# Reordering the first batch of a fused linear-attention and mixture-of-experts kernel

## The chip, the cores and the metric

The kernel runs on one core of one Trainium2 chip. The metric is the device time of one execution in microseconds (us), so lower is better. The core has five engines with a queue each: TensorE for matmuls (PE in the profile, with its weight loads as PEld), VectorE (DVE), ScalarE (ACT), GpSimd (POOL) and SyncE (SP). Work moves between HBM and on-chip memory by DMA transfers, which an engine's queue issues. Every engine goes through its own queue in order.

## The reference, cut to what matters

Attention with a cosine weighting is followed by a mixture of experts whose gates are balanced by eight Sinkhorn steps. Eight batches of eight heads, 576 positions and 64 features each make 4608 tokens of 512 features.

```python
theta = np.pi / 2.0 * pos / S
def phi(x, c, s):
    r = np.maximum(x, 0.0)
    return np.concatenate([r * c, r * s], axis=-1)
q_p, k_p = phi(q, cos_w, sin_w), phi(k, cos_w, sin_w)
kv = np.einsum('bhsf,bhsd->bhfd', k_p, v)       # "key sums with values"
z = np.sum(k_p, axis=2)                         # "key sums"
num = np.einsum('bhsf,bhfd->bhsd', q_p, kv)     # numerators
den = np.einsum('bhsf,bhf->bhs', q_p, z)[..., None] + 1e-06   # denominators
x = num / den                                   # tokens of the experts
...
P = np.exp(x @ w_gate - max)                    # then 8 rounds of row and column scaling
for e in range(E):                              # E = 8
    out += P[:, e:e + 1] * (np.maximum(x @ w1[e], 0.0) @ w2[e])
```

## The kernel before

All matmul operands are 16-bit floats; the loads from HBM convert from 32-bit on the way. The kernel has two phases. In the first, the eight batches go through the attention one by one, and the first expert's two layers run between their pieces, so that TensorE is never without work: block `j` of the first expert handles 512 tokens in 16 slots (eight slots `ffn1`, one for each 128 columns of the first layer, then eight half tiles of `ffn2`), and the table `todo` puts pieces of batch `j + 1` behind the slots. In the second phase the other seven experts run back to back. This change touches only what comes ahead of that regular rhythm: the first batch (batch 0), and the preparation of batch 1 up to slot 4 of block 0.

Work on TensorE, VectorE and ScalarE keeps the order in which the code issues it: each goes through an `InOrder` wrapper (line 109 of the profile, which is why nearly all rows carry L109, and why rows are told apart by their tiles). What a written position says is therefore what the engine does. GpSimd issues the loads of q, k, v and of the weights (`load` at L202, `load_w1` at L127, `load_w2` at L133), in written order too. These issues share eight completion semaphores in turn, so that the ninth and every later issue waits until the issue eight places earlier has landed. Each q, k or v load brings half a batch (two of four head pairs `hk`); the first layer's weights come in four quarters of 256 columns, and so do those of the second layer.

The steps that the prediction names, by function and by the tiles that the profile shows:

- `prep_q(b, hk)`: VectorE scales a head pair's queries by cosine and sine, `q_p<-q_ld,acc_hi` (the table `cs` lives in `acc_hi`). `qp_pool` has three buffers.
- `turn(b, hk, i)`: TensorE transposes a third of it by a matmul with the identity, `small_ps<-ident,q_p`; ScalarE or VectorE writes it to `q_pT` with the relu (for batch 1's last two head pairs the target lies in `acc_lo` and `acc_hi`).
- `prep_k` applies the relu to the keys in place (`k_ld<-k_ld`; by ScalarE for head pairs 0 and 1 of batch 1), `prep_kp` scales them on VectorE (`k_p<-k_ld,acc_hi`).
- `key_sums` sums batch 0's keys by 36 small matmuls from the table `cs_half` (`small_ps<-cs_half,k_ld`), `key_sums_made` spreads them into `zsel`.
- `denominators` multiplies `zsel` with `q_pT` into a bank named `y_ps`; behind head 7, VectorE takes the reciprocal and splits it into two 16-bit parts (`den`, `hi`, `hl`).
- `sums_begun` and `sums_made` sum keys with values (`small_ps<-v_ld,k_p`, then `kv_sb` by ScalarE), two head pairs at a time.
- `spread_out` spreads the reciprocals over the features (`small_ps<-hl,acc_hi`, then `rb` by ScalarE), `numerators` multiplies `q_pT` with `kv_sb`, and VectorE multiplies the product with `rb` into `xT`. `attend` is both.
- the first L1: the first layer of the first 512 tokens for column groups 0 to 3, accumulated over `kt = hk` as the head pairs of `xT` come ready; ScalarE applies the relu into `hT`.
- `keep_busy(n)`: matmuls of ones (dummies) of n times 128 columns, whose result nobody reads.

The banks called `small_ps` are four, used in turn. The order in which the first batch is written (L610 to L638) is this:

```python
for hk in range(HK):
    if hk == 3:
        prep_k(0, 0); prep_k(0, 1)
        z_ps = key_sums(0)
        prep_q(0, hk)
        key_sums_made(0, z_ps)
    else:
        prep_q(0, hk)
    for i in range(3):
        turn(0, hk, i, True)
        keep_busy(3)
```

Behind it stand the scaled keys, the denominators and the sums, and then a loop over `hk` that holds `attend(0, hk)`, the first L1 of the head pair before, and one or two scaled keys of batch 1.

Of the kernel before, what the change touches and what calls it, by code (L numbers as in the profile page):

```python
# [19 lines left out]
XS = 64.0  # L20
# [5 lines left out]
def kernel(  # L26
# [154 lines left out]
    with ExitStack() as p1:  # L181
# [16 lines left out]
        def load(b, half, names="qkv", held_back=False):  # L198
            for name in names:
                x = ld.tile([P, 2, C, D], F16, name=f"{name}_ld")  # L200
                view = sources[name][b].rearrange("(hk hh) (p c) d -> (hh p) hk (c d)", hh=2, c=C)
                i = nc.gpsimd.dma_start(  # L202
                    out=x[:].rearrange("p hk c d -> p hk (c d)"),
                    in_=view[:, 2 * half : 2 * half + 2],
                )
                if held_back:

                    after(ve.last, i)
                landing[name, b, half] = i
                for i in range(2):  # L210
                    loaded[name, b, 2 * half + i] = x[:, i]
# [3 lines left out]
        ve.memset(half_pi[:], float(np.pi / 2.0))  # L215
        ang = float(np.pi / (2.0 * S))
        load(0, 0, "q")
        gidx = cs_pool.tile([P, C], FP32, name="gidx")
        nc.gpsimd.iota(
            gidx[:], pattern=[[1, C]], base=0, channel_multiplier=C,  # L220
            allow_small_or_imprecise_dtypes=True,
        )

        ones_sq = cs_pool.tile([P, P], F16, name="ones_sq")
        ve.memset(ones_sq[:], 1.0)
        ident = cs_pool.tile([P, P], F16, name="ident")
# [1 line left out]
            out=ident[:], in_=ones_sq[:], pattern=[[-1, P]], compare_op=ALU.is_equal,  # L228
            fill=0.0, base=0, channel_multiplier=1,
        )  # L230
        load(0, 1, "q")
        for name in "kv":
            load(0, 0, name)
            load(0, 1, name)
        w0 = new_weights(wA)
        load_w1(w0, 0, 4, (0, 1))
        load(1, 0, "k")
# [7 lines left out]
        def keep_busy(n):  # L245

            for cols in [TCH] * (n // 4) + [n % 4 * P] * (n % 4 > 0):
                te.matmul(
                    out=idle_ps[:, 0:cols],
                    lhsT=ones_sq[:],  # L250
                    rhs=ones_sq[:, 0:1].to_broadcast([P, cols]),
                    start=True,
                    stop=True,
                )

        idle_ps = ps_y.tile([P, Dm], FP32, name="y_ps")
        for _ in range(74):
            keep_busy(1)

        wrap = cs_pool.tile([P, C], FP32, name="wrap")  # L260
# [12 lines left out]
        se.activation(out=cs[:, :, 1, :], in_=s_b, func=AF.Sin, scale=ang)  # L273
        cs_half = cs_pool.tile([P, C, 2, 2], F16, name="cs_half")
        ve.memset(cs_half[:], 0.0)
        for hh in range(2):
            ve.tensor_copy(
                out=cs_half[hh * HP : (hh + 1) * HP, :, :, hh],
                in_=cs[hh * HP : (hh + 1) * HP, :, :, 0],
            )  # L280
        early = cs_pool.tile([P, 1], FP32, name="early")
        se.activation(out=early[:], in_=half_pi[:], func=AF.Exp)

# [3 lines left out]
        for h in range(H):  # L287
            ve.memset(zmask[:, h, h : 32 : H], 1.0)
        C3 = C // 3

        lo = cs_pool.tile([P, 1], FP32, name="lo")

# [4 lines left out]
        with nc.allow_low_precision("sums of zeros and ones"):  # L297
# [8 lines left out]
            out=spread.rearrange("p j hk hh d -> p (j hk hh) d"),  # L306
            in_=sel[:].rearrange("p j h -> p (j h)").unsqueeze(2).to_broadcast([P, 3 * H, D]),
        )
        ones_col = const.tile([P, 1], FP32, name="ones_col")
        ve.memset(ones_col[:], 1.0)  # L310
        ones_all = const.tile([P, P], FP32, name="ones_all")
        ve.memset(ones_all[:], 1.0)
        eps_row = cs_pool.tile([1, 32], FP32, name="eps_row")
        ve.memset(eps_row[:], 1e-6 / XS)
        wg_ld = cs_pool.tile([P, KT, E], FP32, name="wg_ld")
        nc.sync.dma_start(out=wg_ld[:], in_=moe_w_gate.rearrange("(kt p) e -> p kt e", p=P))
        wg = const.tile([P, KT, E], F16, name="wg")
# [2 lines left out]

        kps, qps, qTs, kvs, hls = {}, {}, {}, {}, {}

        lent = acc_lo[:, G_LO - 4 : G_LO, :].rearrange("p g d -> p (g d)").bitcast(F16)
        VA = C * (D + 2)
        v_augs = [
            lent[:, i * VA : (i + 1) * VA].rearrange("p (c d) -> p c d", d=D + 2)
            for i in range(4)
        ]
        q_pTs = [qT_pool.tile([P, C, P], F16, name=f"q_pT{i}")[:] for i in range(6)] + [
            t.rearrange("p (c s) -> p c s", s=P)  # L330
            for t in (
# [1 line left out]
                held[:, held.shape[1] - C * P :],  # L333
            )
        ]
        for t in v_augs:
            ve.memset(t[:, :, D : D + 1], 1.0 / XS)

        def prep_k(b, hk, by_scalar=True):
            k16 = loaded["k", b, hk]  # L340
            if b and by_scalar:
# [4 lines left out]
        def prep_q(b, hk):  # L346

            q16 = loaded.pop(("q", b, hk))
            by_dma = b >= 2
            if by_dma:  # L350
                ve.tensor_scalar(
                    out=q16, in0=q16, scalar1=0.0, scalar2=None, op0=ALU.max
                )
            q_p = qp_pool.tile([P, C, 2, D], F16, name="q_p")
            ve.tensor_tensor(
                out=q_p[:], in0=q16.unsqueeze(2).to_broadcast([P, C, 2, D]),
                in1=cs, op=ALU.mult,
            )
            if by_dma:
                qTs[b, hk] = q_pTs[(b * HK + hk) % len(q_pTs)]  # L360
                turned = nc.sync.dma_start(
                    out=qTs[b, hk], in_=q_p[:].rearrange("p c a d -> p (c a d)"),
                    transpose=True,
                )
                if b == 3 and hk == 0:

                    after(landing["v", b, 1], turned)
            else:
                qps[b, hk] = q_p
# [57 lines left out]
        def key_sums_made(half, z_ps):  # L427

            if half == 0:
                kvs[0] = (  # L430
                    kv_pool.tile([P, HK, 2, D], F16, name="kv_sb"),
                    kv_pool.tile([P, H, 32], F16, name="zsel"),
                )
            ve.scalar_tensor_tensor(
                out=kvs[0][1][:, 4 * half : 4 * half + 4, :],
                in0=z_ps[:, 0:4].unsqueeze(2).to_broadcast([P, 4, 32]),
                scalar=1.0 / XS,
                in1=zmask[:, 4 * half : 4 * half + 4, :],
                op0=ALU.mult,
                op1=ALU.mult,  # L440
            )
# [1 line left out]
        def sums(b, half):  # L443
            sums_made(b, half, sums_begun(b, half))

        def sums_begun(b, half):

            W_ = D + 1 if b else D
            if half == 0 and b:
                kvs[b] = (  # L450
                    kv_pool.tile([P, HK, 2, D], F16, name="kv_sb"),
                    kv_pool.tile([P, H, 32], F16, name="zsel"),
                )
            kv_ps = [ps_s.tile([P, 512], FP32, name="small_ps") for hh in range(2)]
            for i in range(2):
                k_p, v_aug = kps.pop((b, 2 * half + i))
                for c in range(C):
                    for hh in range(2):
                        te.matmul(
                            out=kv_ps[hh][:, i * W_ : (i + 1) * W_],  # L460
                            lhsT=k_p[hh * HP : (hh + 1) * HP, c].rearrange("p a d -> p (a d)"),
                            rhs=v_aug[hh * HP : (hh + 1) * HP, c, 0:W_],
                            start=(c == 0),
                            stop=(c == C - 1),
                        )
            return kv_ps
# [67 lines left out]
        def attend(b, *hks):  # L534
            for hk in hks:
                spread_out(b, hk)
            for hk in hks:
                numerators(b, hk)
# [71 lines left out]
        begun = []  # L610
        epsilons(0)
        for hk in range(HK):
            if hk == 3:
                prep_k(0, 0)
                prep_k(0, 1)
                z_ps = key_sums(0)
                prep_q(0, hk)
                key_sums_made(0, z_ps)
            else:
                prep_q(0, hk)  # L620
            for i in range(3):
                turn(0, hk, i, True)
                keep_busy(3)
        prep_kp(0, 0)
        prep_kp(0, 1)
        denominators(0, range(0, 4))
        keep_busy(8)
        for hk in (2, 3):
            prep_k(0, hk)
        z_ps = key_sums(1)  # L630
        prep_kp(0, 2)
        key_sums_made(1, z_ps)
        prep_kp(0, 3)
        keep_busy(5)
        denominators(0, range(4, 8))
        for half in range(2):
            sums_made(0, half, sums_begun(0, half))
            keep_busy((0, 18)[half])  # L638

        hT = hA.tile([P, FT, TCH], F16, name="hT")  # L640
        first_ps = [
# [1 line left out]
            else ps_y.tile([P, Dm], FP32, name="y_ps")  # L643
            for i in range(4)
        ]
        for hk in range(HK):
            attend(0, hk)
            for kt in ((), (0,), (1,), (2, 3))[hk]:
                for ft, h_ps in enumerate(first_ps):
                    te.matmul(  # L650
                        out=h_ps[:],
                        lhsT=w0[0][:, kt, ft * P : (ft + 1) * P],
                        rhs=xT[:, kt, 0:TCH],
                        start=(kt == 0),
                        stop=(kt == KT - 1),
                    )
                    if kt == KT - 1:
                        se.activation(out=hT[:, ft, 0:TCH], in_=h_ps[:], func=AF.Relu)
            for i in ((), (0,), (1, 2), ())[hk]:
                prep_k(1, i, i < 2)  # L660
            for i in ((), (0,), (1,), (2, 3))[hk]:
                if i == 3:
                    prep_k(1, i, False)
                prep_kp(1, i)
        for hk in range(3):
            prep_q(1, hk)

# [614 lines left out]
```

The softmax here doesn't subtract the row's maximum and nothing guards it: scores larger than these inputs give would overflow.

## Time and profile before

| what | value |
|---|---|
| median of 7 runs | 978.61 us (978.13 to 979.76) |
| the profiled execution, its own time | 978.6 us |
| its span, first to last instruction | 976.9 us |
| PE busy | 961.5 us, 98% of the span |
| DVE, ACT, POOL busy | 807.3, 563.5, 60.7 us |
| granted TensorE clock | 1.000 |
| busy in the first 35 us: PE, DVE, ACT | 31.3, 24.6, 23.0 us |
| what DMA moved from 10 to 40 us | 202 to 207 GB/s in every 5 us |

The span is 1.7 us shorter than the execution's own time; what lies around it is outside the kernel's instructions. A busy PE counts dummies too, so a high share in the first 35 us doesn't say that the work there is useful. In a timeline row the columns are the start in us, the time taken in us (from the first start to the last end of the merged instructions), engine, line, operation with its tiles (out<-in) and shapes, and in square brackets the idle time of the engine ahead of it with what ended it. A row of the DMA view ends with the size of one transfer and the us from its issue to its landing.

### The profile page before, as it was taken

What the parts mean: (1) busy time and instruction counts of PE and PEld (TensorE: products, weight loads), DVE (VectorE), ACT (ScalarE), POOL (GpSimd) and SP (SyncE); (2) the same over time, 40 slices, a digit from 0 to 9 for tenths busy, and PEclk for the clock granted to TensorE, in tenths of its full rate; (3) what the DMA queues carried; (4) which work ended last, traced back from release to release, by engine and by line L of the source; (5) the groups of instructions that cost most, each with busy time, mean ns of one, the idle gap of its engine ahead of it and who ended that gap; (6) DMA issues with size and microseconds to landing.
All of it is one profiled execution on the core that took longest, in us unless ns stands there. A gap on an engine that the chain in (4) does not pass through costs nothing.

```text
span 976.9 us, 20236 instructions
## 1 busy us (share of the span) xinstructions
PE 961.5 (98%) x7855; PEld 674.3 (69%) x7855; DVE 807.3 (83%) x1833; ACT 563.5 (58%) x1262; POOL 60.7 (6%) x82
## 2 busy tenths in 40 slices
PE   9999999999999999999999999999999999999997
PEld 6545555457777777777777777777777777777775
DVE  6767775888988987988888887988888888988887
ACT  5766665477776555555555555555555555555551
POOL 6231110010000000000000000000000000000001
PEclk9999999999999999999999999999999999999999
DMA  9999985330103401323104401323103401104435
GB/s 165 184 150 176 152 141 111 68 68 34 42 26 84 77 25 42 62 56 68 33 26 84 77 25 42 64 53 65 38 26 81 80 25 38 37 26 122 125 89 128
DMA packets 80336, 73.54 MB, mean 75 GB/s; under 512 B 33264, under 2 KB 72176, under 8 KB 80240
## 3 DMA queue, kind: packets, MB, share of 16 engines
q0 software_dynamic: 27232, 30.94, 20.4%
q1 hardware_dynamic: 52768, 41.06, 17.3%
q8 instruction: 61, 1.00, 0.4%
q14 instruction: 35, 0.29, 0.1%
q10 hardware_dynamic: 240, 0.26, 0.1%
HBM read 83.12 MB, written 12.98 MB: 98 GB/s over the span
## 4 chain that ended last, share of the span: by engine, by line
PE 91%; DVE 4%; ACT 2%; DMA 2%; issue 1%; POOL 0%; POOLq 0%; DVEq 0%; ACTq 0%; SPq 0%
PE rows_ps L109 33%; PE h_ps L109 27%; PE p_ps L109 11%; PE copied_ps L109 11%; PE y_ps L109 5%; PE small_ps L109 3%; DMA q_pT<-q_p 1%; DMA acc_hi<-q_p 1%; DVE P_tok L109 1%; ACT q_pT L109 1%; ACT hT L109 0%; DVE colp L109 0%; ACT acc_hi L109 0%; DVE rs L109 0%; DVE acc_hi L955 0%
## 5 line engine op out<-in xcount | busy, mean ns | idle before, releaser
L955 DVE SCALAR_TENSOR_TENSOR acc_lo<-rows_ps,P_tok,acc_lo 128x512 f32<-128x512 f32 (+1 forms) x322 | 203.1, 639 | 75.0 <-PE rows_ps L109 74.9
L109 PEld LDWEIGHTS <-H 128*128 128x128 f16 x2080 | 203.1, 98 | 82.5 <-issue 1.2
L891 ACT CAST u<-h_ps 128x384 f16<-128x384 f32 x288 | 137.5, 478 | 131.2 <-PE h_ps L109 131.2
L109 PEld LDWEIGHTS <-w1e 128*128 128x128 f16 x1632 | 157.7, 98 | 67.8 <-issue 5.4
L885 DVE CUSTOM_DVE_ANT_0 H<-p_ps,u 128x384 f16<-128x384 f32 x329 | 180.8, 550 | 6.6 <-PE p_ps L109 6.6
L109 PEld LDWEIGHTS <-hs 128*128 128x128 f16 x1500 | 146.6, 98 | 56.2
L109 PE MATMUL h_ps<-S,w1e 128*128 128x384 f16 x672 | 164.1, 326 | 0.7 <-ACT u L109 0.6
L109 PE MATMUL p_ps<-xT,T 128*128 128x384 f16 x672 | 164.1, 326 | 0.1
L109 PE MATMUL rows_ps<-V,H 128*128 128x256 f16 x1000 | 150.0, 273 | 0.7 <-DVE acc_hi L955 0.7
L109 PE MATMUL rows_ps<-w2e,hs 128*128 128x256 f16 x1000 | 150.0, 273 | 0.0
L109 PE MATMUL h_ps<-xT,w1e 128*128 128x384 f16 (+1 forms) x616 | 148.7, 350 | 0.4 <-DVE xT L109 0.4
L923 ACT ACTIVATE H<-h_ps 128x384 f16<-128x384 f32 x144 | 70.6, 490 | 95.1 <-PE h_ps L109 95.1
L109 PEld LDWEIGHTS <-T 128*128 128x128 f16 x1008 | 98.5, 98 | 30.1 <-issue 3.6
L109 PE MATMUL rows_ps<-w2e,H 128*128 128x256 f16 (+1 forms) x568 | 92.3, 285 | 0.0
L904 ACT COPY copied_ps<-h_ps 128x384 f32<-128x384 f32 x144 | 67.5, 469 | 35.5 <-PE h_ps L109 35.5
L914 ACT ACTIVATE H<-copied_ps 128x384 f16<-128x384 f32 x144 | 70.8, 492 | 20.4 <-PE copied_ps L109 20.4
L109 PE MATMUL h_ps<-S,T 128*128 128x384 f16 x336 | 81.8, 324 | 0.5 <-ACT copied_ps L109 0.3
L109 PE MATMUL copied_ps<-xT,w1e 128*128 128x384 f16 x336 | 82.1, 326 | 0.0
L109 PE MATMUL copied_ps<-w2e,H 128*128 128x256 f16 x504 | 75.5, 272 | 0.0
L109 PE MATMUL rows_ps<-V,hs 128*128 128x256 f16 x500 | 74.9, 272 | 0.0
L955 DVE SCALAR_TENSOR_TENSOR acc_lo<-copied_ps,P_tok,acc_lo 128x256 f32<-128x256 f32 x126 | 60.0, 476 | 0.6 <-PE copied_ps L109 0.2
L955 DVE SCALAR_TENSOR_TENSOR acc_hi<-rows_ps,P_tok,acc_hi 128x512 f32<-128x512 f32 (+1 forms) x56 | 41.3, 737 | 20.6 <-PE rows_ps L109 19.7
(145 smaller groups left out, 945.6 us busy)
## 6 DMA issues: line engine op xcount, KB each, us to landing
S<-x_saved SPq DMA_DIRECT2D x108, 192.0 KB, 2.4
out_dram<-acc_lo SPq DMA_DIRECT2D x62, 128.0 KB, 2.3
w1e<-in_moe_w_dram POOLq DMA_DIRECT2D x7, 1024.0 KB, 8.7
w2e<-in_moe_w_dram POOLq DMA_DIRECT2D x7, 1024.0 KB, 9.8
q_ld<-in_q_dram POOLq DMA_DIRECT2D x16, 288.0 KB, 6.6
k_ld<-in_k_dram POOLq DMA_DIRECT2D x16, 288.0 KB, 8.1
v_ld<-in_v_dram POOLq DMA_DIRECT2D x16, 288.0 KB, 9.2
x_saved<-S SPq DMA_DIRECT2D x18, 192.0 KB, 1.9
```

Of the source, the lines that this page charges most:

```text
L109: i = getattr(self.engine, name)(*args, **kwargs)
L885: latest = ve._custom_dve(TENSOR_ADD_SAT, out=out, in0=ps[:, 0:TU], in1=t[:], s0=FP32_MAX, s1=0.0)
L891: se.copy(out=t[:], in_=ps[:, 0:TU])
L904: se.copy(out=Y[:, 0:TU], in_=X[:, 0:TU])
L914: se.activation(out=h11, in_=Y[:, 0:TU], func=AF.Relu)
L923: se.activation(out=h12, in_=X[:, 0:TU], func=AF.Relu)
L955: ve.scalar_tensor_tensor(out=a, in0=rows, scalar=P_tok[:, g, self.e : self.e + 1], in1=a, op0=ALU.mult, op1=ALU.add,)
```

## The change

Only the head of the program is rewritten; what is computed stays the same.

- Loads: the second half of batch 0's q is issued directly behind the first, ahead of the iota that the cosine table starts from; the first half of k follows the iota, ahead of the identity's mask. The order of the loads among themselves stays as it was.
- Set-up on VectorE: constants are filled ahead of the two operations that need the identity; the two copies into `cs_half` move behind the second `prep_q`. 55 dummies instead of 74 stand up front.
- Batch 0: all four `prep_q` come ahead of the keys. The keys' relus, key sums, scaled keys and denominators are rearranged so that the reciprocals are taken ahead of the fourth scaled key. The first half of the sums with values and the spreading and numerators of head pair 0 come ahead of the second half of the sums, which goes to `h_ps` banks.
- The first L1 is woven between `spread_out` and `numerators`, which are one head pair apart. The scaled keys of batch 1 all come behind the last numerators of batch 0 on VectorE, and the two relus by ScalarE behind its last `rb` copy.
- Dummies: none behind the transposes of head pair 3, and 4 + 28 + 4 instead of 8 + 5 + 18 units of 128 columns later.

```diff
         load(0, 0, "q")
+        load(0, 1, "q")
         gidx = cs_pool.tile([P, C], FP32, name="gidx")
         nc.gpsimd.iota(
...
+        load(0, 0, "k")
...
-        load(0, 1, "q")
-        for name in "kv":
-            load(0, 0, name)
-            load(0, 1, name)
+        load(0, 1, "k")
+        for half in range(2):
+            load(0, half, "v")
...
-        for _ in range(74):
+        for _ in range(55):
             keep_busy(1)
...
-        for hh in range(2):
-            ve.tensor_copy(
...
+        def halve():
+            for hh in range(2):
+                ve.tensor_copy(
...
-        def sums_begun(b, half):
+        def sums_begun(b, half, banks=(ps_s, "small_ps")):
...
-            kv_ps = [ps_s.tile([P, 512], FP32, name="small_ps") for hh in range(2)]
+            kv_ps = [banks[0].tile([P, 512], FP32, name=banks[1]) for hh in range(2)]
...
         for hk in range(HK):
+            prep_q(0, hk)
+            if hk == 1:
+                halve()
             if hk == 3:
                 prep_k(0, 0)
                 prep_k(0, 1)
                 z_ps = key_sums(0)
-                prep_q(0, hk)
-                key_sums_made(0, z_ps)
-            else:
-                prep_q(0, hk)
             for i in range(3):
                 turn(0, hk, i, True)
-                keep_busy(3)
+                keep_busy(3 * (hk < 3))
         prep_kp(0, 0)
+        key_sums_made(0, z_ps)
+        for hk in (2, 3):
+            prep_k(0, hk)
         prep_kp(0, 1)
         denominators(0, range(0, 4))
-        keep_busy(8)
-        for hk in (2, 3):
-            prep_k(0, hk)
         z_ps = key_sums(1)
+        keep_busy(4)
+        key_sums_made(1, z_ps)
         prep_kp(0, 2)
-        key_sums_made(1, z_ps)
+        denominators(0, range(4, 8))
         prep_kp(0, 3)
-        keep_busy(5)
-        denominators(0, range(4, 8))
-        for half in range(2):
-            sums_made(0, half, sums_begun(0, half))
-            keep_busy((0, 18)[half])
+        sums_made(0, 0, sums_begun(0, 0))
+        keep_busy(28)
+        spread_out(0, 0)
+        numerators(0, 0)
+        keep_busy(4)
+        spread_out(0, 1)
+        sums_made(0, 1, sums_begun(0, 1, (ps_h[0], "h_ps")))
...
+        numerators(0, 1)
+        spread_out(0, 2)
+        first_l1(0, (2, 3, 0, 1))
+        numerators(0, 2)
+        spread_out(0, 3)
+        first_l1(1, range(4))
+        numerators(0, 3)
+        prep_k(1, 0)
+        prep_k(1, 1)
+        first_l1(2, range(4))
+        first_l1(3, range(4))
         for hk in range(HK):
-            attend(0, hk)
-            for kt in ((), (0,), (1,), (2, 3))[hk]:
-                for ft, h_ps in enumerate(first_ps):
-                    te.matmul(
...
-            for i in ((), (0,), (1, 2), ())[hk]:
-                prep_k(1, i, i < 2)
-            for i in ((), (0,), (1,), (2, 3))[hk]:
-                if i == 3:
-                    prep_k(1, i, False)
-                prep_kp(1, i)
+            if hk >= 2:
+                prep_k(1, hk, False)
+            prep_kp(1, hk)
         for hk in range(3):
             prep_q(1, hk)
```

`first_l1(kt, fts)` holds the matmuls and the relu that stood in the loop, for the column groups `fts`.

## The prediction, made before the changed kernel ran

> **What bounds the kernel now.** I read the page first. TensorE is the bound of the program as a whole:
>
> ```profile
> PE 961.5 (98%) x7855; PEld 674.3 (69%) x7855; DVE 807.3 (83%) x1833; ACT 563.5 (58%) x1262; POOL 60.7 (6%) x82
> ```
>
> The change touches only the head, so I went on to the chain of waits in order of time up to 70 us. A gain counts if the head's last link comes earlier; from about 34 us to 58.9 us PE then runs without a wait. Columns: start us, us, what.
>
> ```profile
> 23.30 0.82 DVE xT L109 x2
> 24.12 0.04 issue
> 24.16 0.39 PE h_ps L109
> ...
> 24.57 2.56 ACT hT L109 x5
> ...
> 27.74 0.77 ACT q_pT L109 x2
> ...
> 29.88 1.32 ACT acc_lo L109 x3
> ...
> 33.06 1.03 PE small_ps L109 x54
> ```
>
> From 24.57 to 33.02 us ScalarE is the chain, with hardly a gap; it starts when the last numerators of batch 0 (`xT`, 24.1) allow the end of the first L1. What feeds it next is batch 1's q. The timeline:
>
> ```profile
> 13.38 0.70 POOL L202 DMA_DIRECT2D q_ld<-in_q_dram  x1 [0.64 <-DMA v_ld<-in_v_dram]
> ...
> 20.29 0.68 ACT L109 ACTIVATE k_ld<-k_ld 128x576 f16<-128x576 f16 x1 [0.84 <-DMA k_ld<-in_k_dram]
> ...
> 25.70 2.08 DVE L109 TENSOR_TENSOR q_p<-q_ld,acc_hi 128x1152 f16<-128x1152 f16 x3
> ...
> 26.95 0.67 PE L109 MATMUL small_ps<-ident,q_p 128*128 128x128 f16 x9
> ```
>
> The load issued at 13.38 has this row in the DMA view of that moment (last number: us to landing):
>
> ```profile
> q_ld<-in_q_dram POOLq DMA_DIRECT2D x1, 288.0 KB, 11.9
> ```
>
> So batch 1's first q lands at 13.38 + 11.9 = 25.28 us, and VectorE scales it at 25.70: only 0.42 us later. By the same sum the second half of q lands at 14.83 + 11.9 = 26.73. The table by stage shows that this can't be hurried (last two columns: DMA share, GB/s):
>
> ```profile
> 5.00:10.00 5.00, 4.69 (x67) 3.64 (x65) 3.88 (x23) 2.76 (x8) 4.68 (x6) 1.00 1.09 157
> 10.00:15.00 5.00, 4.89 (x118) 3.25 (x119) 4.49 (x11) 2.83 (x8) 2.37 (x4) 1.00 1.28 202
> 20.00:25.00 5.00, 4.63 (x29) 2.08 (x28) 4.25 (x10) 2.98 (x7) 2.85 (x4) 1.00 1.30 203
> 25.00:30.00 5.00, 4.56 (x41) 2.81 (x40) 4.47 (x8) 4.98 (x12) 2.31 (x4) 1.00 1.23 206
> ```
>
> From 10 us the transfers run flat out, and each issue waits for the landing eight places ahead. Compute that gets ahead by more than about a microsecond runs into q's landing.
>
> [...]
>
> **The change part by part.** Durations are from start to next start where instructions follow closely.
>
> *Set-up.* Nineteen dummies less are worth 19 x 0.053 = 1.0 us of PE, at the pace of 19 starts in the microsecond from 5; but before, PE was free at 6.8 and the first `q_p` ready at 7.6, so they cost nothing. The iota stands behind one more issue of 0.77 us: the cosine table is ready at 5.1 instead of 4.3. VectorE gets through its constants at about 6.0, since the halving (0.5 us) has moved; the first `q_p` starts at about 6.0 instead of 6.8. The second q half is issued 0.44 us earlier, k's first half 0.2, the later loads as before. GpSimd is busy with issues to 9.8 us either way. On SP nothing moves here. The `cs_half` copies now sit where VectorE waits for q's second half (2.61 + 6.2 = 8.8 us), which hides them; without that cover they would cost 0.5.
>
> *Batch 0 to the reciprocals.* k's first half lands at 3.38 + 6.9 = 10.3 us in both. From there VectorE has two relus 0.53, a scaled key 0.67, `zsel` 0.3, two relus 0.5 (k's second half lands at 11.8), a scaled key 0.67, a wait of 0.1 for the key sums (0.73 on PE), `zsel` 0.25, a scaled key 0.67, reciprocal 1.35, `hi` 0.3 and `hl` 0.4: sum 5.7, so `hl` ends at 16.0 instead of 17.42. The fourth query scaling and the fourth key, 1.4 us, have left this stretch. The transposes of head pair 3 wait behind the key sums on PE as before.
>
> *Reciprocals to the end of the first L1.* First `rb` 0.9 after `hl`, so the first numerators' `xT` at 16.9; the next at 18.1, behind 36 sums (0.5) and a spread. Then each head pair needs L1 0.87, spread 0.25 to 0.34 and numerators 0.3 to 0.37 of PE: 1.4 to 1.6. The fourth `xT` starts at 20.9 to 21.3 and ends at 21.7 to 22.1, before 24.1. ScalarE no longer has a key relu that waits for the landing at 20.2 ahead of two `rb` copies. I take 21.7: the chain is 2.4 us ahead here.
>
> *Batch 1's keys.* All four scaled keys and two relus now stand on VectorE behind that: 4 x 0.67 + 2 x 0.33 = 3.34 us, where 1.67 stood before. VectorE is ready for q at 25.0, q lands at 25.28. The first `q_p` is ready at 26.05 and PE starts its transposes at 26.1 instead of 26.95. Queued behind them on PE is L1 group 6, and behind that ScalarE's chain. PE has done groups 4 and 5 by 24.6 and idles for 1.5 us: **of 2.4 us gained, q's landing takes back 1.5**. The second half of q (26.73) lets VectorE's later pieces move by only 0.3, where 1.8 us of slack stood ahead of their transposes; two ScalarE writes lose 0.1 to it. So the v copy that ends ScalarE's chain comes 0.75 earlier.
>
> *What is late next.* Batch 1's v lands at 28.1 and 29.5 (used at 30.4 before), the second layer's quarters at 30.9, 32.2, 33.4 and 34.7 (used from 34.1 and 36.7): all still in time when 0.75 is taken off. Fewer dummies later (36 units against 67 of 128 columns) stand in PE's waits and are worth nothing.
>
> *The unknown* is how the loads' stream moves. While the first load was alone (3 to 4 us) DMA moved 98 GB/s, with two 195. [...] I take 0.05 to 0.1 gained. **Sum:** 0.75 + 0.05 = 0.8 us off 978.6 (the profiled execution's own time: a span of 976.9 and 1.7 around it). The median shown is the same within 0.01, so 977.8.
>
> **Rivals.**
> - *Slower:* the first batch doesn't get ahead, and the keys moved behind it come on top. If the last `xT` still ended at 24.1, `q_p` would start at 27.4 instead of 25.7; PE had 0.45 of slack there, so +1.25 us: 979.9. The turning point is a chain only 1.3 us ahead instead of 2.4. It could come from a half-clocked PE: 9 turns with their dummies take 9 x (3 x 0.057 + 0.163) = 3.0 us at full clock, 6.0 at half. [...]
> - *No change:* the 0.8 is absorbed later. PE waits again between 58.9 and 73.5 us, 1.7 us in all, 0.85 of it for a DMA transposition. The loads still in flight until 43 us don't move with compute. If those waits are DMA's own pace, 978.6. Against it: these transpositions and the loads ahead of them are issued on compute's events, and move with it.
> - *Faster:* the landings don't bind. If the stream came 0.45 earlier, the gain would be 1.2 (977.4); all 2.4 (976.2) would need q 1.5 us earlier, against a queue that is full.
>
> **How the numbers follow.** Main case 0.64, own range 977.3 to 978.3; slower rival 0.14, no change 0.12, faster 0.10. The range 976.9 to 979.5 leaves out a tenth on each side. A measurement tells about 0.2% (2.0 us) from no change, and the main case lies inside that. Faster by more needs nearly the whole lead: 0.09. Slower by more needs the slower rival and a further 0.7 us: 0.08. Within: 0.83.
>
> **What would show it.** In the changed profile: `hl` near 16.0, the last `xT` near 21.7, a new PE idle of 1 to 1.5 us ahead of batch 1's first transposes with VectorE's `q_p` waiting for the q load, and the 54 sums at 32.3 instead of 33.06. A last `xT` after 22.8 would make the slower rival right; q landing before 24.8, the faster; PE 0.8 ahead at 55 us but not at 75, the middle one.

## The result, and the profile after

The changed kernel takes 985.02 us (median; 980.74 to 990.41) where the kernel before takes 978.77 (977.30 to 984.62): a ratio of 1.0060, 95% interval 1.0044 to 1.0075. It is slower by 6.3 us, while 977.8 was predicted. The profiled execution took 983.47 us, its span is 981.7.

The line of busy times and the line of the instruction queue (packets, MB, share) from the page after:

```profile
PE 963.7 (98%) x7833; PEld 674.7 (69%) x7833; DVE 807.5 (82%) x1833; ACT 564.2 (57%) x1262; POOL 60.4 (6%) x82
...
q8 instruction: 61, 1.00, 0.4%
```

PE has 22 matmuls less and is still busy 2.2 us longer: somewhere it ran slower. The second line is easily skipped: 1 MB of instructions is itself moved by DMA, in 61 packets of 16,384 bytes. From the start of the first packet to that of the last, PE ran 15,137 weight loads and matmuls in 60 steps, 252 each (15,204 and 253 in the kernel before); 256 to a packet is my estimate from these.

The timeline of PE after, around the sums of keys with values:

```profile
13.54 0.51 PE L109 MATMUL y_ps<-q_pT,zsel 128*32 128x192 f16 x12
13.98 0.46 PE L109 MATMUL small_ps<-v_ld,k_p 64*128 64x64 f16 x19
16.41 0.42 PE L109 MATMUL small_ps<-v_ld,k_p 64*128 64x64 f16 x17 [1.97 <-issue]
16.77 3.09 PE L109 MATMUL y_ps<-ones_sq 128*128 128x512 f16 x7
19.65 0.69 PE L109 MATMUL small_ps<-hl,acc_hi 96*128 96x192 f16 x3
```

The 36 sums are one unbroken loop, and yet PE stops after the nineteenth for 1.97 us. The releaser is "issue": it waited for nothing that the profile shows. Seven dummies then take 3.09 us; the same seven take 1.69 where the clock is full. Only at 19.65 come the spreads of the reciprocals, though these were ready long before. VectorE's timeline shows both ends of that:

```profile
15.77 0.41 DVE L109 SCALAR_TENSOR_TENSOR hl<-hi,lo,den 96x192 f16<-96x192 f16 x1
16.11 0.75 DVE L109 TENSOR_TENSOR k_p<-k_ld,acc_hi 128x1152 f16<-128x1152 f16 x1
20.73 0.56 DVE L109 TENSOR_TENSOR xT<-small_ps,rb 128x384 f16<-128x384 f32 x1 [3.88 <-PE small_ps L109]
```

`hl` ends at 16.18 as predicted (16.0); the first `xT` starts at 20.73 instead of the predicted 16.9. A second loss lies later. The tables by stage (PE busy comes first; the column of 0.69 is the granted clock), then the timeline of PE, then that of ScalarE:

```profile
15.00:20.00 5.00, 3.59 (x27) 1.63 (x26) 1.78 (x4) 0.43 (x2) 2.75 (x4) 0.69 1.32 202
65.00:70.00 5.00, 5.00 (x25) 2.01 (x23) 2.76 (x7) 3.13 (x8) 0.00 (x0) 0.69 0.90 134
```

```profile
64.69 0.64 PE L109 MATMUL small_ps<-hl,acc_hi 96*128 96x192 f16 x3 [2.51 <-ACT rb L109]
65.29 0.69 PE L109 MATMUL small_ps<-q_pT,kv_sb 128*64 128x384 f16 x4
65.91 2.96 PE L109 MATMUL y_ps<-w2e,hT 128*128 128x512 f16 x8
```

```profile
63.10 0.68 ACT L109 ACTIVATE k_ld<-k_ld 128x576 f16<-128x576 f16 x1 [3.65 <-DMA k_ld<-in_k_dram]
63.70 0.57 ACT L109 COPY acc_lo<-y_ps 128x512 f32<-128x512 f32 x1
64.16 0.70 ACT L109 COPY rb<-small_ps 128x384 f32<-128x384 f32 x2
```

ScalarE stands 3.65 us at a key relu of batch 3 that waits for its load; PE's spreads wait for the `rb` copy queued behind it, idle 2.51 us, and then PE runs at half clock again. By the trace's clock record the half-clocked stretches (granted 0.5) are 16.89 to 20.30 and 64.67 to 68.08, each 3.41 us, and from the one start to the other it is 47.78 us, 14 times that. Their length and this distance suggest windows of 3.41 us. PE was not idle throughout the two windows ahead: it was busy for 40% and 27% of them, as the table by stage shows (PE busy first):

```profile
13.48:16.89 3.41, 1.38 (x49) 1.04 (x50) 3.30 (x6) 0.03 (x1) 1.88 (x3) 1.00 1.40 201
61.26:64.67 3.41, 0.93 (x4) 0.30 (x4) 0.13 (x1) 1.56 (x4) 0.00 (x0) 1.00 1.24 127
```

The sum for this execution, by marks in the trace (after minus before): `hl` -1.25; from there to the first `xT` +3.61; first to last `xT` -0.15; last `xT` to the second layer's first matmul (`y_ps<-w2e,hT`, 37.67 against 34.03) +1.43, together +3.64. From there to the gates of block 2 (80.52 against 75.48) +1.40, and to the end -0.18: 4.86, the difference of the spans. This execution is 1.5 us shorter than the median one, so these marks place a good part of the 6.3 us and not all of it.

### The profile page after: what moved, and what is told of

Same layout as the page of the kernel before. It is cut to its first block, busy times and chain, and to the rows that moved or that the text cites. A ratio compares the mean times of both kernels' runs of the same rounds, so it can differ in the third digit from the quotient of the medians.

```text
span 981.7 us, 20192 instructions
## 1 busy us (share of the span) xinstructions
PE 963.7 (98%) x7833; PEld 674.7 (69%) x7833; DVE 807.5 (82%) x1833; ACT 564.2 (57%) x1262; POOL 60.4 (6%) x82
## 4 chain that ended last, share of the span: by engine, by line
PE 89%; DMA 4%; DVE 3%; issue 3%; ACT 1%; POOL 1%; POOLq 0%; ACTq 0%; SPq 0%
PE rows_ps L109 33%; PE h_ps L109 26%; PE p_ps L109 11%; PE copied_ps L109 11%; PE y_ps L109 4%; PE small_ps L109 3%; DMA k_ld<-in_k_dram 1%; DMA w2e<-in_moe_w_dram 1%; DMA w1e<-in_moe_w_dram 1%; DVE P_tok L109 1%; DVE colp L109 0%; POOL q_ld L202 0%; DVE rs L109 0%; DVE acc_hi L971 0%; DVE rr L109 0%
```

## The experiments

Sixteen kernels ran. "Pause" below is the profiled PE's idle time ended by "issue", "second layer" its first matmul in us. Instructions are counted along PE's program, weight loads included, so that a dummy counts as two. A ratio, and a difference of medians, is taken against executions of the kernel before in the same session (its medians were 978.41 to 979.17).

### First question: the order, or the dummies?

The expectations weigh three theories: the new order itself, too few dummies for the clock, and the fetch of PE's instructions. For the fetch the profile after gives 6.15 us from instruction 192 (10.26) to instruction 448 (16.41): 3.7 until a packet starts between them, 0.95 for the packet, 1.5 behind it. That this packet hangs on instruction 192, and that the 6.15 us hold in other kernels, is my estimate.

**Wide dummies** (e1), the same columns in 19 dummies:

```diff
-        for _ in range(55):
-            keep_busy(1)
+        for n in (4,) * 12 + (1,) * 7:
+            keep_busy(n)
```

> The changed kernel with its 55 dummies up front issued as 12 of 512 and 7 of 128 columns: the same columns in 72 fewer TensorE instructions. [...] With 72 fewer, the two places lie 72 instructions later: 192 at about 11.3, so ready at 17.4, and 448 in the second half of the sums, due at about 17.6: no stall, no half clock at 17 us, first xT near 17, last xT near 21.7 to 22.1, the 54 sums near 32.3, and a time of 977.5 to 979. Order theory (the new order itself is slow, the stall only a symptom): the dummies' form changes nothing, 984 to 986. Clock theory (too few dummies cooled TensorE): the columns are the same, so no change either, 984 to 986.

980.97 us (977.24 to 988.37), ratio 1.0019 [1.0004, 1.0034]. No pause, `hl` at 15.86, second layer at 33.76. The new order by itself doesn't stop PE. But the median lies above the 977.5 to 979 that I gave: with the head as expected, 6 of 22 executions still exceed 982 us.

**74 dummies in the new order** (e2; `range(55)` back to `range(74)`):

> The changed kernel with the 74 dummies of before up front. Fetch theory: 38 more instructions bring the places 38 instructions forward: instruction 192 near 9.1 (TensorE starts the transposes 0.6 later), ready near 15.3, and 448 due near 13.9: a stall of about 1.3 instead of 2.15 us, so a part of the loss remains, 979 to 983. Clock theory: the dummies were what was missing, no half clock, 977 to 979. Order theory: 984 to 986.

979.89 us (978.95 to 982.32), ratio 1.0012 [1.0001, 1.0023]: it is 1.5 us above before, so 4.8 of the 6.3 us are back. No pause at all, where I had expected one, and the second layer at 33.56.

**55 dummies in the old order** (e3; `range(74)` to `range(55)`):

> The kernel before with only 55 dummies up front and nothing else changed. Fetch theory: 192 moves to a place that runs at 10.7, ready at 16.85, and 448 to one that is due at 15.4, in the first half of the sums: a stall of about 1.5 us where there was none; behind it stand 18 units of dummies, so the first spreading starts about 1.2 us late, and the half clock may follow: 979.2 to 983. Order theory: nothing hangs on these dummies, 978.5 to 979. Clock theory: a little slower by colder matmuls, but no stall in the sums.

984.33 us (978.12 to 988.08), ratio 1.0048 [1.0027, 1.0069]. This one line makes nearly the whole loss. The timeline of its PE, where the profiled execution was one of the shorter ones (979.06):

```profile
15.31 0.37 PE L109 MATMUL small_ps<-v_ld,k_p 64*128 64x64 f16 x13
16.56 1.03 PE L109 MATMUL small_ps<-v_ld,k_p 64*128 64x64 f16 x59 [0.88 <-issue]
```

The same kind of pause stands in the same loop, but after the thirteenth sum.

**Without the 28 units of dummies behind the sums** (e4; the changed kernel less `keep_busy(28)`):

> The changed kernel without the 28 units of dummies (seven matmuls) between the first half of the sums and the first spreading. Fetch theory: the stall stays (2.15 us, ends near 16.4), but the spreading no longer waits behind dummies at half clock (16.8 to 19.7) and starts near 16.9; the last xT comes 2 to 3 us earlier, near 23.5, and the time falls by 2 to 3 us to 981 to 983; the half clock itself remains and slows the L1. Order theory: 984 to 986, since the loss lies in the keys behind the numerators. Clock theory: fewer dummies make the half clock longer, 985 to 988.

983.16 us (978.87 to 988.70), ratio 1.0047 [1.0031, 1.0063]. The pause is 2.02 us and the half clock stays, so taking dummies off the path cures neither. It does shorten what follows: the first `xT` comes at 18.00 instead of 20.73 and the second layer at 35.91 instead of 37.67, for the 28 units had stood between the pause and the spreads. The median falls by 1.5 us.

### Second question: their number, or the warmth that they give?

**74 narrow dummies with the columns of 55**, in the new order (f1) and in the old one (f2):

```diff
-        for _ in range(55):
-            keep_busy(1)
+        for cols in [P] * 36 + [D] * 38:
+            te.matmul(out=idle_ps[:, 0:cols], lhsT=ones_sq[:], ...)
```

> The new order, with 74 dummies up front that together cover the columns of 55 (36 of 128 columns and 38 of 64). Count theory (the number of TensorE instructions ahead of the work decides, because it decides which instruction TensorE has not yet got when it needs it): no pause of 1 us or more among the sums of keys with values, no half-clocked dummies at 17 to 20 us, first matmul of the second layer at 33.5 to 34.1 us, about 979.9 us and a ratio near 1.001, as with 74 full dummies in the new order. Warmth theory (too few columns of dummies, so TensorE is colder): a pause and half clock as in the changed kernel, 983 to 986 us, ratio near 1.006. Order theory (the rearrangement itself): likewise 985.

> The old order, with 74 dummies up front that together cover the columns of 55. Count theory: nothing changes for the instructions behind, so 978.4 to 979.0 us, ratio within 0.1% of 1. Warmth theory: about 984, as with 55 full dummies in the old order (ratio 1.0048).

New order: 979.36 us (978.30 to 981.39), ratio 1.0009 [1.0001, 1.0017]. Old order: 978.72 us (977.78 to 980.29), ratio 0.9999 [0.9991, 1.0007]. PE's timeline in the first, with nothing between the sums:

```profile
14.18 0.70 PE L109 MATMUL small_ps<-v_ld,k_p 64*128 64x64 f16 x36
14.81 1.69 PE L109 MATMUL y_ps<-ones_sq 128*128 128x512 f16 x7
16.45 0.42 PE L109 MATMUL small_ps<-hl,acc_hi 96*128 96x192 f16 x3
```

**The converse: 55 dummies with the columns of 74** (g1), old order:

```diff
-        for _ in range(74):
-            keep_busy(1)
+        for n in (2,) * 19 + (1,) * 36:
+            keep_busy(n)
```

> The old order with 55 dummy instructions up front that cover the columns of 74 (19 of 256 and 36 of 128 columns), the converse of the 74 narrow ones. Count theory: TensorE pauses for about 1 us at its instruction 448, within the first sums of keys with values, and the median is 983 to 985 us, as with 55 plain ones (984.3), although TensorE does as many columns as before. Warmth theory: no loss, 978.4 to 979.

982.04 us (978.26 to 988.57), ratio 1.0033 [1.0018, 1.0048]: slow, with as many columns as before. Together with f1 and f2 this says that the number decides. The rise is 3.1 us here and was 5.9 with 55 plain dummies; the two intervals overlap, so whether the columns add something isn't settled. From PE's timeline of its profiled execution (985.31 us):

```profile
16.77 1.03 PE L109 MATMUL small_ps<-v_ld,k_p 64*128 64x64 f16 x59 [0.82 <-issue]
...
77.83 0.51 PE L109 MATMUL small_ps<-acc_hi,zsel 128*32 128x192 f16 x6 [4.55 <-DMA acc_hi<-q_p]
78.26 3.59 PE L109 MATMUL h_ps<-xT,w1e 128*128 128x512 f16 x8
```

**64 dummies in the new order** (g2):

> The new order with 64 dummies up front. Count theory: instruction 192 runs near 9.3 us, its 16 KB packet ends near 13.6 and instruction 448 runs at 15.0 to 15.5, so the pause is 1.0 to 1.3 us instead of 2.0; the median lies between those of 74 and of 55 dummies, 981 to 984 us. If only the order counted, 985; if any number above some small one were enough, 979.9.

979.60 us (978.92 to 980.42), ratio 1.0001 [0.9990, 1.0011]. The pause is 0.34 us, shorter than expected, and the median is below the 981 to 984 that I gave: the loss doesn't grow evenly as dummies are taken away.

What the number does is seen in the packets. In all eighteen traces, before and after included, a packet starts 1.8 to 4.1 us after PE's instruction 192 has run, takes 0.9 us, and each pause in the table stands ahead of instruction 448, 256 later:

| kernel | up front | instr. 192 ran | packet ended | 448 ran | pause |
|---|---|---|---|---|---|
| before | 74 | 8.76 | 13.04 | 14.95 | none |
| after | 55 | 10.26 | 14.94 | 16.41 | 1.97 |
| new order | 74 | 8.28 | 11.56 | 13.52 | none |
| new order | 64 | 10.01 | 13.62 | 15.04 | 0.34 |
| old order | 55 | 10.35 | 15.04 | 16.56 | 0.88 |
| old order, columns of 74 | 55 | 10.39 | 15.37 | 16.77 | 0.82 |
| new order, wide | 19 | 10.91 | 14.91 | 17.22 | none |

Where PE pauses, instruction 448 runs 1.4 to 1.5 us after its packet has ended, in eight traces of eight; where it doesn't, 1.8 us or more. So PE ran out of instructions and waited for a packet, which moved beside loads of 202 GB/s. Where it asks for that packet the traces don't show; I took the place 256 ahead of 448. It may lie somewhat earlier: by the same count, 44 of the 61 packets in the trace of before start ahead of the instruction that would ask for them, by up to 1.8 us. From 192 to the packet's end and 1.4 to 1.5 us behind it, where by my estimate PE can run on, it takes 4.1 to 6.5 us in all. What the dummies' number changes is the work that lies in between: it lasts 6.1 to 6.7 us in the old order with 74 and 5.0 to 5.6 with 55, in the new order 5.2 to 5.9 and (without g3 below, which moves dummies into it) 4.2 to 4.5, because fewer dummies push both numbers on into a stretch where PE waits less.

### Third question: is the half clock a matter of how busy a window is?

16 of the 28 units of dummies go ahead of the first sums (g3):

```diff
+        keep_busy(16)
         sums_made(0, 0, sums_begun(0, 0))
-        keep_busy(28)
+        keep_busy(12)
```

> The changed kernel, 16 of its 28 units of dummies ahead of the first sums of keys with values instead of behind them. The fetch is as late as before, so instruction 448 still runs near 16.4 us, but the pause ahead of it shrinks to 1.0 to 1.3 us, and the window of 13.5 to 16.9 us is busy for about 2.2 of its 3.4 us. Theory that a window less than half busy halves the clock: no half clock at 17 to 20 us, first xT at 18.4 to 18.9 us instead of 20.73, median 982 to 983.5. Theory that the pause itself, of whatever length, or the missing instructions bring the half clock: first xT near 20.5, median 985.

980.75 us (979.02 to 987.22), ratio 1.0027 [1.0012, 1.0043]. PE's timeline:

```profile
13.64 1.04 PE L109 MATMUL y_ps<-ones_sq 128*128 128x512 f16 x4
14.62 0.40 PE L109 MATMUL small_ps<-v_ld,k_p 64*128 64x64 f16 x15
16.01 0.48 PE L109 MATMUL small_ps<-v_ld,k_p 64*128 64x64 f16 x21 [0.99 <-issue]
16.42 0.82 PE L109 MATMUL y_ps<-ones_sq 128*128 128x512 f16 x3
17.09 0.41 PE L109 MATMUL small_ps<-hl,acc_hi 96*128 96x192 f16 x3
...
77.19 0.51 PE L109 MATMUL small_ps<-acc_hi,zsel 128*32 128x192 f16 x6 [3.65 <-DMA acc_hi<-q_p]
```

The dummies fill a part of the time that was pause, the three behind it run at full clock (0.82 us), and the first `xT` comes at 17.96 instead of 20.73. That gain isn't the half clock's alone, for there are also four dummies less between the sums and the spreads: e4, at half clock and with none there, has its first `xT` at 18.00. The half clock's own price is 1.4 us on the seven dummies (3.09 against 1.69), and e4's second layer comes 1.1 us later than this one's.

The theory of the window holds beyond this run. The clock records of the eighteen traces put all windows on a grid of 3.41 us. Each of the 24 windows at full clock that PE filled to 40% or less was followed by half clock, fifteen of them at the end of a program; of the few between 44% and 47% some were and some weren't; none above 47% was. So half a clock followed a pause of 2 us where one window held nearly all of it, in the two traces that have one (after and e4); a pause of 0.99 us is at most 29% of a window. But at 77.19 PE waits 3.65 us, and the slowest executions stay.

### Fourth question: where does the rest come from?

The head doesn't explain it. With 55 dummies in the old order the second layer is only 0.7 us late (34.74), and the median rises by 5.9. The 64 dummies and the 16 + 12 units have the same head (second layer at 34.81 and 34.83), yet none of 13 executions of the first exceeds 982 us, and 7 of 19 of the second do. Counted together, 49 of 90 executions exceed 982 us where 55 dummies stand up front (after, e3, e4, g1, g3), 5 of 105 where 74 or 64 do (e2, f1 to f4, g2, g4), and 9 of 210 of the kernel before; with the 19 wide ones 6 of 22.

Between 57 and 80 us I saw two places. The first is the key relu. **ScalarE's two relus of batch 3's keys one slot later**, in the new order with 74 dummies (f3) and in the old (f4):

```diff
-  (8, prep_k, 0), (8, prep_q, 2),
-  (9, prep_k, 1), (10, prep_kv, 0), (10, prep_k, 2)
+  (8, prep_q, 2), (9, prep_k, 0),
+  (10, prep_k, 1), (10, prep_kv, 0), (10, prep_k, 2)
```

> The new order with 74 dummies, and ScalarE's relus of batch 3's keys for head pairs 0 and 1 one slot later, each behind the reciprocal copies of the head pair that they stood ahead of. Theory that the 0.4 us gained in the head are lost where those relus wait for their load (1.55 us of TensorE at 57.7): that idle goes, 977.9 to 978.6 us, ratio 0.9995 to 1.0000. Theory that the loss lies elsewhere (the transpositions by DMA for batch 3 at 67 to 73 us, 2.2 us there): the idle at 57.7 goes but the later ones stay or grow, 979.3 to 980.3, ratio near 1.001.

> The old order with its 74 dummies, the same two relus one slot later. In the old order only 0.27 us of TensorE's idle hung on them in the profiled execution, so 978.0 to 978.6 us in the median, ratio 0.9993 to 1.0002; if slower executions are made by these relus, their highest times come down from 983 to below 981. If the new order's head is worth its 0.4 us, the new order with the same move is 0.4 us faster than this; if not, equal or slower.

New order: 980.12 us (978.58 to 983.41), ratio 1.0017 [1.0009, 1.0026]. Old order: 978.97 us (977.49 to 980.74), ratio 0.9997 [0.9989, 1.0005]. PE's wait for `rb` near 59 us is gone in both profiles, and other waits stand in its place: 1.53 at 68.71 for VectorE and 0.85 for the transposition in the new order, 0.57 and 3.11 in the old. With 74 dummies that relu is not where the time is to be had; with 55, where it cost PE 2.51 us in the profile after, the move wasn't tried.

The second place is the wait for `acc_hi<-q_p`, batch 3's last transposition by DMA. In the profiles with 74 or 64 dummies it costs PE 0.72 to 3.11 us; with 55 it costs 4.55, 3.65 and 6.09 (g1, g3, e4), 1.07 in the short execution of e3, and nothing in the profile after, where the time was lost at 64.69. PE runs at half clock behind the three long ones, as the `x8` at 78.26 shows (3.59 us for eight, 1.89 at full clock). **No transposition by DMA**: TensorE transposes all batches, in both orders, with both numbers (j1 to j4).

```diff
-                turned = nc.sync.dma_start(out=qTs[b, hk], ..., transpose=True)
+            qps[b, hk] = q_p
...
+                    if fn is prep_q:
+                        for i in range(3):
+                            at(j, slot + 1, turn, b + 1, hk, i)
```

> The old order with 74 dummies; the queries of batches 2 to 7 are transposed by TensorE one slot behind their scaling, as those of batches 0 and 1 are, so no transposition by DMA is left. 24 head pairs at 0.5 us of TensorE and the waits for their copies: 990 to 1010 us. It is the base for the next three.

> The same with 55 dummies up front. Transposition theory (the larger part of the loss needs batch 3's transposition by DMA): the head's delay alone, 0.4 to 1.2 us above the one with 74. Theory that a late head makes the later loss by itself: 3 to 6 us above it.

> The new order with 74 dummies and no transposition by DMA. Batch 1's keys behind the numerators give back what the earlier reciprocals gain: within 1.0 us of the old order with 74.

> The changed kernel (55 dummies) with no transposition by DMA. The head still has its pause of 2 us and the half clock: 3.0 to 4.2 us above the new order with 74 if the later part needs the transposition, 5 to 7 us if not. If the head were not the place of the loss, 0 to 1 us.

Old order 1008.90 and 1009.86 us (74 and 55), new order 1009.39 and 1010.81; their ratios to before are 1.0299 [1.0285, 1.0314], 1.0315 [1.0296, 1.0335], 1.0303 [1.0287, 1.0319] and 1.0327 [1.0311, 1.0344]. So 55 instead of 74 cost 1.0 and 1.4 us here, against 5.9 and 4.8 with the transpositions; with four or five executions each these two are rough. The pauses are still there; the old order's:

```profile
15.04 0.37 PE L109 MATMUL small_ps<-v_ld,k_p 64*128 64x64 f16 x13
16.29 0.89 PE L109 MATMUL small_ps<-v_ld,k_p 64*128 64x64 f16 x49 [0.88 <-issue]
```

The new order's is 0.85 us in its profile, without a half clock, so it is no measure of the 3.64 us of the profile after; I had expected 3.0 to 4.2. As far as so few executions tell, the larger part of the loss went with the transpositions; the intervals of 74 and 55 overlap, and leave room for more. These kernels are 30 us slower and have other waits, and three of the four (not j4) run at half clock from about 39.5 to 43 us, which no other kernel does. So this supports the second place rather than proves it.

What links the number of dummies with a wait at 77 us isn't settled. Nineteen dummies less shift all later packets as well: in four of the five traces with 55 an instruction packet comes at 63.9 to 65.0 us, beside the second of batch 3's four transpositions, and in the fifth at 68.3, where that transposition starts at 68.4; with 74 or 64 it comes at 58.4 to 63.2. SyncE's issues show what goes with it, first in before and then in g1:

```profile
63.87 1.29 SPq L361 DMA_TRANSPOSE q_pT<-q_p  x1
65.27 1.30 SPq L361 DMA_TRANSPOSE acc_lo<-q_p  x1
66.75 1.46 SPq L361 DMA_TRANSPOSE acc_hi<-q_p  x1
```

```profile
64.47 1.55 SPq L361 DMA_TRANSPOSE q_pT<-q_p  x1
66.14 1.29 SPq L361 DMA_TRANSPOSE acc_lo<-q_p  x1
67.61 1.56 SPq L361 DMA_TRANSPOSE acc_hi<-q_p  x1
```

From the second transposition to the third it is 1.55 to 1.67 us in all five traces with 55, and 1.40 or 1.41 in the nine others that have transpositions. In g1, g3 and e4 the last one is thereby issued 0.18 to 0.31 us behind the first of batch 4's loads, and these are the three long waits; in the others it comes from 1.18 us ahead of that load to 0.16 behind. That the packet holds up an issue, and the loads then overtake the last transposition, fits these times. It can't be all: f4 waits 3.11 us, though its last transposition is issued only 0.12 us behind and no packet comes there. Restoring the later positions by nineteen tiny matmuls at 32 us, or releasing batch 4's loads a slot later, would have tested it; neither was run on the chip.

### Fifth question: what is the new order worth?

With 74 dummies it should have been faster by the 0.8 us of the prediction, and it was slower by 0.1%. **Batch 1's keys at their old places** (g4), everything else as in the new order with 74 dummies:

```diff
         numerators(0, 1)
+        prep_k(1, 0)
+        prep_kp(1, 0)
         spread_out(0, 2)
...
         numerators(0, 2)
+        prep_k(1, 1)
+        prep_k(1, 2, False)
+        prep_kp(1, 1)
         spread_out(0, 3)
...
-        for hk in range(HK):
-            if hk >= 2:
-                prep_k(1, hk, False)
-            prep_kp(1, hk)
+        prep_kp(1, 2)
+        prep_k(1, 3, False)
+        prep_kp(1, 3)
```

> The new order with 74 dummies, but batch 1's relus and scaled keys at their old places between the numerators of batch 0. Theory that the keys' new place is what lets batch 0's chain get ahead (no relu that waits for k's landing at about 20.2 us ahead of the reciprocal copies): the last xT ends near 23.5 us instead of 22.3, and the first matmul of the second layer comes at 33.8 to 34.3 instead of 33.56; the median is 979.5 to 980.5. Theory that the keys' new place costs what the new order with 74 dummies loses against the old (1.2 us): median 978.4 to 979.0.

978.35 us (977.50 to 980.84), ratio 0.9995 [0.9988, 1.0002]. VectorE behind the last numerators, first in the new order with 74 dummies, then here:

```profile
21.35 0.87 DVE L109 TENSOR_TENSOR xT<-small_ps,rb 128x384 f16<-128x384 f32 x2 [0.76 <-PE small_ps L109]
22.14 1.42 DVE L109 TENSOR_TENSOR k_p<-k_ld,acc_hi 128x1152 f16<-128x1152 f16 x2
...
25.51 2.08 DVE L109 TENSOR_TENSOR q_p<-q_ld,acc_hi 128x1152 f16<-128x1152 f16 x3
```

```profile
22.94 0.81 DVE L109 TENSOR_TENSOR xT<-small_ps,rb 128x384 f16<-128x384 f32 x2
23.67 0.75 DVE L109 TENSOR_TENSOR k_p<-k_ld,acc_hi 128x1152 f16<-128x1152 f16 x1
24.34 0.30 DVE L109 TENSOR_SCALAR k_ld<-k_ld 128x576 f16<-128x576 f16 x1
24.67 0.76 DVE L109 TENSOR_TENSOR k_p<-k_ld,acc_hi 128x1152 f16<-128x1152 f16 x1
25.35 2.09 DVE L109 TENSOR_TENSOR q_p<-q_ld,acc_hi 128x1152 f16<-128x1152 f16 x3
```

Two scaled keys instead of four stand between the last `xT` and the first `q_p`. The stretch from the start of the last `xT` to the second layer is 10.26 to 10.28 us in every trace with the keys at their old places, and 11.68 to 11.80 in every trace with them behind: 1.4 us or a little more, whatever else happens. What the earlier reciprocals bring is of the same size: with no pause, `hl` ends at 15.73 to 17.28 in the new order (mean of four 16.3) and at 17.43 to 18.05 in the old (mean of three 17.7). The second layer comes at 34.2 in the mean in the one and at 34.05 in the other, so the move gains nothing. Of all kernels here this one has the lowest median, though against before its interval takes in 1.

## Why the prediction was wrong, point by point

- **The failed step** is "Nineteen dummies less ... cost nothing", and with it "Fewer dummies ... are worth nothing". It counted the dummies' time on PE, which is indeed free, and not their number. The 55 alone cost 5.9 us in the old order, and restoring 74 gave back 4.8 of 6.3 in the new: PE ran out of instructions at its instruction 448 for 1.97 us, half a clock followed, and 28 units of the later dummies stood in the path and not in a wait. In the profile after, that is 3.6 of the 4.9 us. How the number brings the losses behind 55 us is not shown. The list of what is moved left out one queue: that of PE's own instructions.
- **`hl` at 16.0**: right, 16.18. **Last `xT` at 21.7**: wrong for the kernel as changed (it ends near 26.3), right for its order in one profile with 74 dummies (22.2) and not in another (23.8): `hl` alone varies by over a microsecond between profiles, and the prediction rested on one.
- **Batch 1's keys, 3.34 us on VectorE**: right in size (22.14 to 25.51 is 3.37). That q's landing takes back 1.5 us was the wrong releaser: `q_p` follows the last scaled key directly, and its start kept its distance from the last `xT` in the profile after too (3.64 us), long after q had landed. The keys are the bound there. PE's wait ahead of the transposes was foreseen at 1 to 1.5 us and is 1.08.
- **The sum of -0.8**: for the order with 74 dummies the medians are 0.7 to 1.5 us above those of before. The terms that were mis-sized are the lead, 1.3 us in the mean at the last `xT` and not 2.4, and what is taken back of it, all and not 1.5 of 2.4. That leaves about 1 us behind 34 us; it goes when the keys go back, and why isn't explained. No run shows the 0.05 us taken for the loads' stream; in the profile after, batch 1's first q half landed at 13.47 + 10.8 = 24.27 us, 1.0 us earlier than before, and VectorE came to scale it at 29.62.
- **All shifts together after 34 us**: wrong. From the second layer's first matmul to the gates of block 2 the profiles take 40.5 to 47.8 us, for work that is the same.
- **The slower rival** named the right sign and even a half-clocked PE. In the profile after, half a clock followed a pause of 1.97 us in the sums, in a window that PE filled to 40%, and the pause had a cause that no rival had. The rival's price, +1.25, was a fifth of the loss.

## What to carry to other kernels

Dummy instructions were also spacing here: in the new order the profiles with 74, 64 and 55 of them pause for 0, 0.34 and 1.97 us ahead of the same instruction 448. So change their number and their width separately, and look at "issue" gaps in an unbroken loop before blaming the order around it. A lead that was gained ahead of a block of work in order on one engine was worth only what that block left (1.3 us gained in the mean ahead of batch 1's keys, 1.4 given back behind them); measure the distance from the block to the next stage in both versions first. Where a kernel waits for DMA at many places, one profile of each version isn't enough to price a microsecond: the same wait took PE 0 to 6.09 us.

## What the runs showed of the hardware

- PE's instructions came over DMA in packets of 16,384 bytes (61 in before and in after, 253 and 252 instructions apart in the mean); the one ahead of instruction 448 ended 2.7 to 5.0 us after instruction 192 had run, beside a load stream of about 200 GB/s. Where PE had to wait for it, in eight traces, instruction 448 ran 1.4 to 1.5 us after the packet's end.
- Of the windows of 3.41 us in eighteen traces, all 24 that PE filled at full clock to 40% or less were followed by half a clock, and none that it filled to more than 47%.
- Beside an instruction packet, one DMA transposition to the next took 1.55 to 1.67 us in SyncE's issues (five traces) instead of 1.40 or 1.41 (nine traces).
- The wait for the same DMA transposition was between 0 and 6.09 us in profiles of kernels whose work at that place is identical.
